# Moving two matmul operands by 64 and 128 bytes in SBUF

## The chip, the core and the metric

The kernel runs on one core of a Trainium2 chip. The metric is the time on the device in microseconds, from the first to the last work of the program; the median of three runs is given. A profile of one further execution shows what each engine did.

## The reference

The inputs are q, k and v with 8 batches, 12 heads, 448 positions and a head size of 64, and two weight matrices of 768 x 2048 and 2048 x 768. Attention uses a sigmoid instead of a softmax, so that rows need no normalisation, and a dense layer with GELU follows:

```python
scores = q @ k.T / sqrt(64) - log(448)
attn   = 1 / (1 + exp(-scores))
x      = (attn @ v)                      # heads side by side: 3584 tokens x 768
h      = x @ w_in                        # 3584 x 2048
g      = 0.5 * h * (1 + erf(h / sqrt(2)))
out    = g @ w_out                       # 3584 x 768
```

## The kernel before, in words

**Precision.** Most products are made of three matmuls each. An operand a is split into a high part, rounded to the type fp32r, and a low part a - high. The product is then low weights x high operand, high weights x low operand, and high x high, summed in PSUM. The first batches' attention is computed with plain fp32 matmuls instead.

**Tiling.** The eight batches are processed as seven rounds: each round has the 448 tokens of one batch and 64 tokens of the remaining batch (`TOK`), 512 columns in all. A round has two stages on TensorE. In the expansion (`ffn1`, with `hidden`, lines 428 to 430) 16 output tiles are made, each out of 6 chunks of x, three matmuls per chunk: 288 matmuls of 128 x 128 weights against 128 x 512 operands. Over seven rounds each of the three lines has 672. The moving operands are `xh[:, cc]` and `xl[:, cc]`. ScalarE applies GELU twice (lines 445 and 446) and VectorE subtracts, which gives the high and low part of `g[fc]`. In the projection (`ffn2`, lines 477 to 479) 6 output tiles are made, each out of 16 tiles of g, three matmuls per tile: again 288 a round and 672 per line over all. There the moving operands are `g[fc][:, 0]` and `g[fc][:, 1]`.

**Order.** The program is written out by hand; each engine works in the order in which the code issues. `window` weaves the attention of a coming batch between the projection's matmuls, so that a few scores matmuls (lines 289 and 294, or 340 in the fp32 form) or values matmuls (386, or 356), of 448 columns, stand between runs of projection matmuls. The expansion stages have no attention between them, and neither has the projection of the last round.

**Weights.** They come from DRAM as 64-bit floats and are decoded on VectorE and ScalarE in the first round, into the tiles that g takes later (`w_in`) and into `wst`; they are then stored in scratch as fp32 and loaded again by SyncE's queue in every later round. `prepare_to` splits a unit of weights into `whl` with a cast on ScalarE (line 226) and a subtraction on VectorE (line 227). Each matmul has its own 128 x 128 weights, a slice of `whl`, loaded by TensorE while the matmul before it runs.

**Places in SBUF.** Each of the 128 partitions is one range of bytes, and the pools put their tiles into it one behind the other. The pool `const` holds, in this order, `one` (32 bytes), `xh` and `xl` (12288 bytes each) and the 16 tiles of g (4096 bytes each); the pool `sb` with everything else follows, `whl` and all of attention's tiles among it. Apart from `one` every size is a multiple of 256 bytes. In the built program x, g, the weights and attention's operands therefore all start at byte 160 of a block of 256. A tile asked for under a tag that is already known takes the buffer of that tag.

Of the kernel before, what the change touches and what calls it, by code (L numbers as in the profile page):

```python
# [9 lines left out]
F32 = mybir.dt.float32  # L10
# [7 lines left out]
P = 128  # L18
# [4 lines left out]
def tile_sigmoid_attention_gelu_ffn(  # L23
# [15 lines left out]
    NF, _, NC, _ = w_in.shape  # L39
# [13 lines left out]
    const = ctx.enter_context(tc.tile_pool(name="const", bufs=1))  # L53
# [3 lines left out]

    ctx.enter_context(tc.manual_schedule())

    one = const.tile([P, 8], F32, name="one")[:, :1]  # L60
    xh = const.tile([P, NPAIR, T], F32R, name="xh")
    xl = const.tile([P, NPAIR, T], F32R, name="xl")
    g, first_w = {}, {}

    def g_tile(fc, name, dtype=F32R):
        return const.tile([P, 2, T], dtype, tag=f"g{fc}", name=name)

    scr_in = tc.dram_tile([NF, P, NC * P], F32, name="scr_in")
    scr_out = tc.dram_tile([NO, P, NFH * P], F32, name="scr_out")
    scr_x = tc.dram_tile([2, P, NPAIR, S], F32, name="scr_x")  # L70
# [511 lines left out]
```

## Time and profile before

| | |
|---|---|
| median of 3 runs | 1219.84 us (1219.82 to 1221.88) |
| profiled execution, its own time | 1225.91 us |
| its span, first to last instruction | 1224.1 us |
| TensorE busy with matmuls | 1210.4 us |
| TensorE busy with weight loads | 961.8 us |
| ScalarE, VectorE busy | 815.5 us, 769.2 us |
| granted TensorE clock | 0.998 |
| DMA, mean rate | 141 GB/s |

PE is TensorE with its matmuls, PEld its weight loads, which run beside the matmuls; DVE is VectorE, ACT is ScalarE, POOL is GpSimd, SP is SyncE, which issues most of the transfers. A row of a group gives the line, the engine and the operation, out<-in, the shapes and the count, then busy time in us, the mean of one in ns, and the idle time before them. A matmul's duration reaches from its start to its last result; since matmuls are pipelined these durations overlap, and the distance from start to start says how fast they follow each other. A row of the timeline gives the start in us from the first instruction, the duration in us, and the instruction.

### The profile page before, as it was taken

To read this page: it belongs to the slowest core of one execution; us is meant where nothing else is said; L and a number is where in the kernel's file an instruction comes from. 1 tells how busy PE (TensorE), PEld (TensorE's weight loads), DVE (VectorE), ACT (ScalarE), POOL (GpSimd) and SP (SyncE) were. 2 spreads that over 40 slices of the span, in tenths; PEclk is the share of its full clock that TensorE was granted. 3 is DMA by queue.
4 is the path that set the end of the run, shared out by engine and by line. 5 is a ranking of instruction groups with operands and counts; after the bars stand their busy time and mean duration, and the time that the engine had idled before them with its cause. 6 is when DMAs were issued, how large, how long until landed. Compare 5 with 4: busy or idle time off the path is not lost.

```text
span 1224.1 us, 15057 instructions
## 1 busy us (share of the span) xinstructions
PE 1210.4 (99%) x5448; PEld 961.8 (79%) x5448; DVE 769.2 (63%) x1127; ACT 815.5 (67%) x1247; POOL 8.6 (1%) x18
## 2 busy tenths in 40 slices
PE   8999999999999999999999999999999999999998
PEld 4338866668888888888888888888888888888887
DVE  4777788623589734798445896447984378953420
ACT  7886576534699744899546997459984489954421
POOL 0000000000000000000000000000000000000000
PEclk9999999999999999999999999999999999999999
DMA  8994567524443135442244432345422544223330
GB/s 278 300 283 153 183 214 246 183 82 154 154 140 113 57 104 174 150 143 73 91 157 147 142 108 76 123 145 162 133 69 87 172 148 147 78 82 104 131 114 26
DMA packets 79881, 172.23 MB, mean 141 GB/s; under 512 B 24256, under 2 KB 39616, under 8 KB 79808
## 3 DMA queue, kind: packets, MB, share of 16 engines
q1 hardware_dynamic: 78080, 164.99, 42.4%
q0 software_dynamic: 1728, 6.29, 1.3%
q8 instruction: 43, 0.70, 0.2%
q14 instruction: 30, 0.25, 0.1%
HBM read 144.90 MB, written 26.35 MB: 140 GB/s over the span
## 4 chain that ended last, share of the span: by engine, by line
PE 95%; DMA 3%; DVE 1%; ACT 1%; SPq 0%; issue 0%; DVEq 0%; ACTq 0%
PE po L477 13%; PE po L478 13%; PE po L479 12%; PE ph L428 12%; PE ph L429 12%; PE ph L430 12%; PE pav L386 7%; PE sc L294 6%; PE pav L356 3%; PE sc L340 3%; DMA raw_ring<-w_in_dram 1%; PE sc_l L289 1%; DMA raw<-w_in_dram 1%; DMA qr<-q_dram 1%; DVE me_ring L117 0%; SPq L328 0%
## 5 line engine op out<-in xcount | busy, mean ns | idle before, releaser
L477 PE MATMUL po<-g,whl 128*128 128x512 f32 x672 | 263.3, 392 | 0.0
L478 PE MATMUL po<-g,whl 128*128 128x512 f32 x672 | 262.3, 390 | 0.0
L479 PE MATMUL po<-g,whl 128*128 128x512 f32 x672 | 261.9, 390 | 0.0
L428 PE MATMUL ph<-xh,whl 128*128 128x512 f32 x672 | 261.5, 389 | 0.0
L429 PE MATMUL ph<-xl,whl 128*128 128x512 f32 x672 | 261.4, 389 | 0.0
L430 PE MATMUL ph<-xh,whl 128*128 128x512 f32 x672 | 261.4, 389 | 0.0
L227 DVE TENSOR_TENSOR whl<-wst,whl 128x768 fp32r<-128x768 f32 (+1 forms) x168 | 179.6, 1072 | 65.1 <-ACT whl L226 61.9
L447 DVE TENSOR_TENSOR g<-gf,g 128x512 fp32r<-128x512 f32 x112 | 77.5, 692 | 212.0 <-ACT g L446 211.8
L445 ACT ACTIVATE gf<-ph 128x512 f32<-128x512 f32 x112 | 66.9, 597 | 199.4 <-PE ph L430 185.5
L226 ACT CAST whl<-wst 128x768 fp32r<-128x768 f32 (+1 forms) x168 | 155.4, 928 | 5.5 <-PE po L479 4.2
L477 PEld LDWEIGHTS po<-g,whl 128*128 128x128 f32 x672 | 126.2, 188 | 31.9 <-issue 8.1
L428 PEld LDWEIGHTS ph<-xh,whl 128*128 128x128 f32 x672 | 126.1, 188 | 26.9 <-issue 0.7
L479 PEld LDWEIGHTS po<-g,whl 128*128 128x128 f32 x672 | 126.1, 188 | 26.8
L430 PEld LDWEIGHTS ph<-xh,whl 128*128 128x128 f32 x672 | 126.1, 188 | 26.2
L429 PEld LDWEIGHTS ph<-xl,whl 128*128 128x128 f32 x672 | 126.1, 188 | 26.1
L478 PEld LDWEIGHTS po<-g,whl 128*128 128x128 f32 x672 | 126.2, 188 | 23.8
L314 ACT ACTIVATE a<-sc 128x896 f32<-128x896 f32 (+1 forms) x174 | 128.3, 786 | 17.3 <-PE sc L340 8.3
L308 DVE TENSOR_TENSOR al<-a,ah 128x896 fp32r<-128x896 f32 x120 | 97.8, 855 | 35.4 <-ACT ah L307 35.4
L307 ACT CAST ah<-a 128x896 fp32r<-128x896 f32 x120 | 85.7, 754 | 5.6 <-PE pav L386 4.2
L386 PE MATMUL pav<-ah,vs 128*128 128x448 f32 x240 | 87.7, 365 | 0.0
L294 PE MATMUL sc<-qs,ks 128*128 128x448 f32 x360 | 82.9, 366 | 0.0
L294 PEld LDWEIGHTS sc<-qs,ks 128*128 128x128 f32 x360 | 67.6, 188 | 6.8
(60 smaller groups left out, 1210.4 us busy)
## 6 DMA issues: line engine op xcount, KB each, us to landing
wst<-scr_in SPq DMA_DIRECT2D x96, 384.0 KB, 3.1
wst<-scr_out SPq DMA_DIRECT2D x72, 512.0 KB, 3.3
kr<-k_dram SPq DMA_DIRECT2D x30, 448.0 KB, 4.3
vr<-v_dram SPq DMA_DIRECT2D x48, 256.0 KB, 4.6
out_dram<-ob SPq DMA_DIRECT2D x42, 224.0 KB, 2.0
raw_ring<-w_in_dram SPq DMA_DIRECT2D x11, 768.0 KB, 7.0
raw_ring<-w_out_dram SPq DMA_DIRECT2D x16, 512.0 KB, 4.7
qr<-q_dram SPq DMA_DIRECT2D x36, 224.0 KB, 3.2
```

The lines of the kernel that those rows point to most:

```text
L226: nc.scalar.copy(hl[:, 0, :w], t[:, :w])
L227: nc.vector.tensor_tensor(hl[:, 1, :w], t[:, :w], hl[:, 0, :w], op=ALU.subtract)
L294: nc.tensor.matmul(o, ks[:, keys], qs, start=n == 0, stop=n == 1)
L308: nc.vector.tensor_tensor(al[t][:, c], a[t][:, c], ah[t][:, c], op=ALU.subtract)
L314: nc.scalar.activation(a, sc, AF.Sigmoid, bias=NEG_LOG_S, scale=SCALE)
L386: nc.tensor.matmul(pav[:, :S], vs[:, j, c], a, start=n == 0, stop=n == len(terms) - 1)
L428: nc.tensor.matmul(ph, wl, xh[:, cc], start=cc == 0, stop=False)
L429: nc.tensor.matmul(ph, wh, xl[:, cc], start=False, stop=False)
L430: nc.tensor.matmul(ph, wh, xh[:, cc], start=False, stop=cc == NC - 1)
L477: nc.tensor.matmul(po, wl, g[fc][:, 0], start=first, stop=False)
L478: nc.tensor.matmul(po, wh, g[fc][:, 1], start=False, stop=False)
L479: nc.tensor.matmul(po, wh, g[fc][:, 0], start=False, stop=last)
```

## The change

`one` is taken from a tile of 96 bytes instead of 32. Behind `xl` a tile of 64 bytes is asked for which nobody uses. The 16 tiles of g are asked for at once, under the tags that the later requests use, so that they lie directly behind that gap. Another unused tile of 128 bytes follows. In the built program x stands at byte 224 of a block of 256 and g at byte 32, while the weights and all other operands stay at 160; everything in the pool `sb` lies 256 bytes further on. On each engine and queue the same instructions stand in the same order as before; only their addresses, the buffers' numbers and the line numbers (five more behind the edit) differ.

```diff
-    one = const.tile([P, 8], F32, name="one")[:, :1]
+    one = const.tile([P, 24], F32, name="one")[:, :1]
     xh = const.tile([P, NPAIR, T], F32R, name="xh")
     xl = const.tile([P, NPAIR, T], F32R, name="xl")
+
+    const.tile([P, 16], F32, name="gap_g")
     g, first_w = {}, {}
 
     def g_tile(fc, name, dtype=F32R):
         return const.tile([P, 2, T], dtype, tag=f"g{fc}", name=name)
 
+    for fc in range(NF):
+        g_tile(fc, f"g_place{fc}")
+    const.tile([P, 32], F32, name="gap_w")
     scr_in = tc.dram_tile([NF, P, NC * P], F32, name="scr_in")
```

## The prediction

> **What bounds the kernel now.** I read the page's head and its chain of waits first, to see whether one engine sets the end.
>
> ```profile
> span 1224.1 us, 15057 instructions
> PE 1210.4 (99%) x5448; PEld 961.8 (79%) x5448; DVE 769.2 (63%) x1127; ACT 815.5 (67%) x1247; POOL 8.6 (1%) x18
> PE 95%; DMA 3%; DVE 1%; ACT 1%; SPq 0%; issue 0%; DVEq 0%; ACTq 0%
> ```
>
> TensorE stands for 95% of the chain that ended last, and nothing else holds more than 3% of it. A change that touches neither the number of matmuls nor their order can move the time only through the distance from one matmul's start to the next. The groups of instructions say which matmuls weigh most.
>
> ```profile
> L477 PE MATMUL po<-g,whl 128*128 128x512 f32 x672 | 263.3, 392 | 0.0
> L478 PE MATMUL po<-g,whl 128*128 128x512 f32 x672 | 262.3, 390 | 0.0
> L479 PE MATMUL po<-g,whl 128*128 128x512 f32 x672 | 261.9, 390 | 0.0
> L428 PE MATMUL ph<-xh,whl 128*128 128x512 f32 x672 | 261.5, 389 | 0.0
> L429 PE MATMUL ph<-xl,whl 128*128 128x512 f32 x672 | 261.4, 389 | 0.0
> L430 PE MATMUL ph<-xh,whl 128*128 128x512 f32 x672 | 261.4, 389 | 0.0
> ```
>
> Six groups of 672, 4032 matmuls in all, stream x (L428 to L430) or g (L477 to L479) past weights from whl: exactly the three tensors whose places change. The last column is zero, so they never wait. Their 390 ns overlap one another and are not what one costs. The cost is the distance between starts, and the timeline of TensorE shows it, here around one head of attention in the second window.
>
> ```profile
> 399.68 0.39 PE L478 MATMUL po<-g,whl 128*128 128x512 f32 x1
> ...
> 401.27 0.39 PE L479 MATMUL po<-g,whl 128*128 128x512 f32 x1
> 401.49 0.36 PE L289 MATMUL sc_l<-qs,ks 128*128 128x448 f32 x1
> 401.69 1.38 PE L294 MATMUL sc<-qs,ks 128*128 128x448 f32 x6
> 402.91 0.39 PE L477 MATMUL po<-g,whl 128*128 128x512 f32 x1
> 403.14 0.40 PE L478 MATMUL po<-g,whl 128*128 128x512 f32 x1
> 403.38 0.39 PE L479 MATMUL po<-g,whl 128*128 128x512 f32 x1
> 403.61 0.39 PE L477 MATMUL po<-g,whl 128*128 128x512 f32 x1
> 403.83 0.39 PE L478 MATMUL po<-g,whl 128*128 128x512 f32 x1
> ```
>
> From 399.68 to 401.27 there are seven steps (1.59 us, 227 ns each). The seven matmuls of 448 columns take 1.42 us from 401.49 to 402.91 (203 ns each), the first of them 200 ns. The three 512-column steps right behind attention take 0.70 us (402.91 to 403.61, 233 ns each) before the fourth is back at 220 to 230. So the same matmul on the same operands costs 227 ns in one moment and 233 ns in another.
>
> Is another engine behind that? The windows by stage say no: here the second expansion (264.9 to 330.2), the window behind it, and the last projection, which has no attention beside it.
>
> ```profile
> 264.90:330.20 65.30, 65.30 (x289) 54.05 (x288) 29.01 (x36) 32.94 (x53) 0.00 (x0) 1.00 0.44 144
> 330.20:429.90 99.70, 99.70 (x458) 85.64 (x457) 82.30 (x130) 86.95 (x136) 0.00 (x0) 1.00 0.36 114
> 1155.00:1220.10 65.10, 65.10 (x289) 53.87 (x287) 12.50 (x11) 13.49 (x17) 0.00 (x0) 1.00 0.26 85
> ```
>
> Columns are length, busy PE, PEld, DVE, ACT, POOL, then granted clock, DMA share and GB/s. Both the expansion and the last projection hold 288 matmuls: 65.3/288 = 227 ns and 65.1/288 = 226 ns, though VectorE and ScalarE are busy 29 and 33 us in one and 13 and 13 us in the other, and DMA 0.44 against 0.26. The clock is 1.00 in all three. What makes 227 or 233 ns is therefore inside TensorE, between its two readings of SBUF: the moving operand, and the weights of the next matmul. The timeline of weight loads shows how these lie together.
>
> ```profile
> 399.91 0.19 PEld L477 LDWEIGHTS po<-g,whl 128*128 128x128 f32 x1
> 400.14 0.19 PEld L478 LDWEIGHTS po<-g,whl 128*128 128x128 f32 x1
> ```
>
> The load at 399.91 starts with the third matmul of that stretch (399.68 plus 0.23) and lasts 0.19 of its 0.227 us. So each weight load lies under the matmul before it, from its start, and ends some 37 ns ahead of the next start: at 512 columns the load itself is not the bound.
>
> **The change part by part.** The first tile grows by 64 bytes, which moves xh and xl by 64. A gap of 64 bytes ahead of g moves g by 128. A gap of 128 behind g moves everything later by 256, so weights, attention's tiles and staging keep their place modulo 256. No instruction, wait or transfer is added, removed or reordered, on any engine or queue. The gaps are never written, and the placeholders for g share the buffers that g takes later. These cost nothing, and no cover is needed for it, because nothing is issued.
>
> What can change is the step of the 4032 matmuls above, 2016 with x and 2016 with g. The trace has no matmul whose operands stand at different places modulo 256, because all their tiles begin at one place and their slices step by multiples of 256. So I bound the step from both sides.
>
> From below: the 448-column step of 200 ns against 227 ns for 512 columns gives 27/64 = 0.42 ns per column. 512 columns at 0.42 are 216 ns, and 11 ns per matmul are left over. If that whole rest were the two readings disturbing one another, and the new places ended it, 4032 x 11 ns = 44 us would go. From above: the dearest step that the same matmul shows in a run is 233 ns, 6 ns more, and 4032 x 6 ns = 24 us would come. The ends are -44 and +24 us, 1176 and 1244 us against the median.
>
> [...]
>
> Which value between? That the steps behind attention rise to 233 ns and fall back by themselves, without a wait, says that the relative timing of the two readings costs something. Since one reading walks through addresses as time goes on, a shift in address is much like a shift in time, so the places should matter. But the moving operand passes through 256 bytes in 64 columns, 64 x 0.42 = 27 ns, and so goes round some seven times under one 0.19 us load: a new starting place moves the moments of meeting more than their number. I therefore take neither end, but half of the 11 ns, and in one of the two stages only, because x and g now stand a quarter and a half of the 256 bytes away and it is unlikely that both are equally good. That is 2016 x 5.4 ns = 10.9 us.
>
> Would the gain arrive? In the window from 330.2 to 429.9 the next busiest engine is ScalarE with 86.95 of 99.7 us. Even the full 11 ns on its 288 matmuls takes 3.2 us away and leaves 96.5 us, still 9 us more than ScalarE works. So it stays TensorE's, and the transfers (0.36 of the time) have room too.
>
> The profiled execution took 1225.91 us, with a span of 1224.1 us and 1.8 us around it, and lies 6 us above the median of 1219.84. The differences here are per step, so I take them from the median: 1219.84 - 10.9 = 1209 us.
>
> **The rivals.** *Nothing changes.* The two readings may not meet by address at all: the 11 ns may be a fixed cost of a change of weights, and the 233 ns an after-effect of the shorter steps of attention. For it: the 227 ns are the same to a nanosecond over whole stages while the slices of weights and operands change. Against it: all those slices stand at the same place modulo 256, so this sameness tests nothing below 256 bytes. Time: 1219.84 us.
>
> The Trainium skill's page "SBUF — State Buffer", section "Who interferes with whom", stands on this side: TensorE has two independent read ports, one for the moving operand and one for weights, and waits for nobody. By that rule the sum would be zero and the time 1219.84. The trace agrees as to the other engines (227 and 226 ns with much and little work beside); on the two ports against each other no run here decides.
>
> *The new places are worse.* The steady 227 ns is the lowest step that 512 columns show; every disturbed one is dearer. If the common place is a lucky one, in which the weights' reading runs behind the moving one without touching it, then any shift leads into the 233 ns. This is settled in the stages of L428 and L477 themselves: in both, it costs 24 us (1244), in one alone 12 us (1232). It decides as soon as the mean step over both stages is above 227.7 ns (0.6 ns x 4032 = 2.4 us). Against it: the step recovers to 227 within four matmuls, so TensorE settles rather than drifts, and might settle at new places too.
>
> *Better in one stage, worse in the other.* With 11 ns saved in one (22 us) and 6 ns lost in the other (12 us) the time is 1210, near my own. With 5.4 saved and 6 lost it is 1221, no change.
>
> That the change misses its aim is shut out by the sizes in the diff: 32 to 96 bytes for the first tile, 64 and 128 for the gaps, all operands by a whole number of floats.
>
> **How the numbers follow.** Differences up to 0.2%, 2.4 us, cannot be told from no change in this kernel. My forecast of faster has 0.44, no change 0.26, slower 0.30 (half of it in one stage, half in both). The likeliest case alone would lie from 1190 to 1217. The range of 1188 to 1240 leaves out the last quarter of the lower bound, about 0.06, and the full 233 ns in both stages, about 0.08.
>
> **What would show it.** In the profile after, the starts of L428 to L430 in an expansion stage and of L477 to L479 in the last projection give the two steps at once: 65.3 and 65.1 us for 288 matmuls each, now. Forecast: one of them falls to about 63.7 us (221 ns) and the other stays. No change: both stay within 0.2 us. Slower: one or both near 67 us. The steps of attention (203 ns) must not change, since its operands keep their common place. If those move as well, or if the two stages stay and the time still changes, the step between the matmuls was the wrong place to look.

## The result: 1.5% slower, and the profile after

The changed kernel takes 1238.62 us (median of four runs, 1237.59 to 1239.33) against 1220.31 us before: a ratio of 1.0147, with a 95% interval of 1.013 to 1.0165. The forecast of 1209 us was wrong in its sign. The time lies between the two prices given for the rival "the new places are worse" (1232 for one stage, 1244 for both).

The head of the page of the changed kernel, with its chain of waits:

```profile
span 1235.8 us, 15057 instructions
PE 1225.8 (99%) x5448; PEld 963.3 (78%) x5448; DVE 770.2 (62%) x1127; ACT 816.2 (66%) x1247; POOL 8.8 (1%) x18
PE 97%; ACT 2%; DMA 0%; issue 0%; SPq 0%; ACTq 0%
```

The same instructions, and the other engines have the same work (VectorE 770.2 against 769.2 us, ScalarE 816.2 against 815.5). Only TensorE has become busier, by 15.4 us. The windows by stage answer to those of before; the columns are length, busy PE, PEld, DVE, ACT, POOL, clock, DMA share and GB/s. They are the second expansion, the window behind it and the last projection:

```profile
261.10:327.00 65.90, 65.90 (x289) 54.07 (x288) 28.99 (x36) 33.06 (x53) 0.00 (x0) 1.00 0.45 143
327.00:428.70 101.70, 101.70 (x457) 85.81 (x457) 82.41 (x130) 87.00 (x136) 0.00 (x0) 1.00 0.36 112
1165.00:1231.90 66.90, 66.90 (x289) 54.08 (x287) 12.50 (x11) 13.49 (x17) 0.00 (x0) 1.00 0.25 83
```

The expansion grew from 65.3 to 65.9 us (x, 64 bytes), the last projection from 65.1 to 66.9 (g, 128 bytes), and the window with attention in it from 99.7 to 101.7. The timeline of TensorE around one head of attention shows it matmul by matmul (start in us, duration):

```profile
573.74 0.39 PE L482 MATMUL po<-g,whl 128*128 128x512 f32 x1
...
574.89 0.40 PE L484 MATMUL po<-g,whl 128*128 128x512 f32 x1
575.13 0.37 PE L294 MATMUL sc_l<-qs,ks 128*128 128x448 f32 x1
575.34 1.40 PE L299 MATMUL sc<-qs,ks 128*128 128x448 f32 x6
576.58 0.39 PE L482 MATMUL po<-g,whl 128*128 128x512 f32 x1
```

Five projection steps take 1.15 us (230 ns each), the step into attention 0.24, and the seven steps of attention 1.45 us (575.13 to 576.58), where they took 1.42 before, although none of attention's operands has moved against its weights. Where the same seven stand behind an expansion stage, they still take 1.41 us in this trace (327.05 to 328.46), as they did before (1.41 us):

```profile
326.82 0.39 PE L435 MATMUL ph<-xh,whl 128*128 128x512 f32 x1
327.05 0.36 PE L294 MATMUL sc_l<-qs,ks 128*128 128x448 f32 x1
327.25 1.38 PE L299 MATMUL sc<-qs,ks 128*128 128x448 f32 x6
328.46 0.39 PE L482 MATMUL po<-g,whl 128*128 128x512 f32 x1
```

So it is what runs ahead of a seven that makes it dearer.

To sum up over the whole kernel I took all distances from start to start of the two traces, group by group. From the first expansion matmul to the last start of all,

| steps | number | before, ns | after, ns | more, us |
|---|---|---|---|---|
| expansion to expansion | 2009 | 226.7 | 229.0 | 4.5 |
| projection to projection | 1882 | 228.5 | 232.8 | 8.2 |
| projection into attention | 115 | 226.7 | 238.5 | 1.4 |
| within attention's sevens | 720 | 202.1 | 206.7 | 3.3 |
| the rest | | | | 0.1 |

Together that is 17.5 us, which is the whole difference between these two points of the traces: 1128.1 us before, 1145.6 us after. Their ends can be read from the groups' first and last starts, before and then after:

```profile
L428 PE MATMUL ph<-xh,whl x672: 389/389/500, 91.9 to 1154.3; 128*128 128x512 f32 x168
L479 PE MATMUL po<-g,whl x672: 388/389/398, 159.7 to 1220.1; 128*128 128x512 f32 x168
```

```profile
L433 PE MATMUL ph<-xh,whl x672: 388/388/501, 86.1 to 1164.4; 128*128 128x512 f32 x168
L484 PE MATMUL po<-g,whl x672: 390/393/404, 154.5 to 1231.7; 128*128 128x512 f32 x168
```

From 91.9 to 1220.1 before, from 86.1 to 1231.7 after. (In the earlier profile the first expansion began 6 us later. Of its chain of waits 3% are transfers, where the later one has 0%, and its granted clock is 0.95 from 60 to 92 us, where the later one has 1.00. These 6 us ahead of the first expansion are why the two spans differ by 11.7 us only.)

### The profile page after: what moved, and what is told of

Its sections match the earlier page's. It is cut to its first block, busy times and chain, and to the rows that moved or that the text cites. A ratio compares the mean times of both kernels' runs of the same rounds, so it can differ in the third digit from the quotient of the medians.

```text
span 1235.8 us, 15057 instructions
## 1 busy us (share of the span) xinstructions
PE 1225.8 (99%) x5448; PEld 963.3 (78%) x5448; DVE 770.2 (62%) x1127; ACT 816.2 (66%) x1247; POOL 8.8 (1%) x18
## 4 chain that ended last, share of the span: by engine, by line
PE 97%; ACT 2%; DMA 0%; issue 0%; SPq 0%; ACTq 0%
PE po L482 13%; PE po L483 13%; PE po L484 13%; PE ph L435 13%; PE ph L434 12%; PE ph L433 12%; PE pav L391 7%; PE sc L299 6%; PE sc L345 4%; PE pav L361 4%; PE sc_l L294 1%; ACT a L319 1%; ACT me_ring L135 0%; ACT me_ring L138 0%; DMA qk<-k_dram 0%; ACT a_last L319 0%
## 5 line engine op out<-in xcount | busy, mean ns | idle before, releaser
L482 PE MATMUL po<-g,whl 128*128 128x512 f32 x672 | 266.0, 396 | 0.0
L483 PE MATMUL po<-g,whl 128*128 128x512 f32 x672 | 265.5, 395 | 0.0
L484 PE MATMUL po<-g,whl 128*128 128x512 f32 x672 | 265.4, 395 | 0.0
L450 ACT ACTIVATE gf<-ph 128x512 f32<-128x512 f32 x112 | 66.9, 597 | 203.0 <-PE ph L435 188.8
```

Source lines behind the costliest of these rows:

```text
L482: nc.tensor.matmul(po, wl, g[fc][:, 0], start=first, stop=False)
L483: nc.tensor.matmul(po, wh, g[fc][:, 1], start=False, stop=False)
L484: nc.tensor.matmul(po, wh, g[fc][:, 0], start=False, stop=last)
```

## Experiments: the two shifts apart, and together with the weights

*x alone*, 64 bytes. g goes back to the weights' place:

```diff
-    const.tile([P, 16], F32, name="gap_g")
+    const.tile([P, 48], F32, name="gap_g")
-    const.tile([P, 32], F32, name="gap_w")
```

> x stands 64 bytes further on, g keeps the weights' place modulo 256. Theory (each stage pays for its own operand's place): the expansion's step is about 229.2 ns as in the changed kernel, the projection and attention go back to the values of before; 2016 x 2.4 ns = 5 us above the kernel before, about 1225 us. Rival (the two shifts act together, for instance through the writes of g and the reads of x): the time stays near 1238 us or goes back to 1220 us.

Measured: 1226.24 us against 1221.81 of the kernel before beside it, ratio 1.0039 (1.0024 to 1.0054). Its expansion and its last projection:

```profile
259.60:325.50 65.90, 65.90 (x289) 54.09 (x288) 29.00 (x36) 32.95 (x53) 0.00 (x0) 1.00 0.45 143
1153.60:1218.70 65.10, 65.10 (x288) 53.87 (x287) 12.50 (x11) 13.50 (x17) 0.00 (x0) 1.00 0.26 85
```

*g alone*, 128 bytes:

```diff
-    one = const.tile([P, 24], F32, name="one")[:, :1]
+    one = const.tile([P, 8], F32, name="one")[:, :1]
-    const.tile([P, 16], F32, name="gap_g")
+    const.tile([P, 32], F32, name="gap_g")
```

> g stands 128 bytes further on, x keeps the weights' place. Theory (each stage for itself): the projection's step is about 232 to 233 ns, the steps of attention that stand between projection matmuls are 4 ns dearer as in the changed kernel, the expansion goes back to 226.7 ns: about 13 us above the kernel before, 1233 us. Rival (acting together): 1220 or 1238 us.

Measured: 1236.07 against 1221.81 us, ratio 1.0113 (1.0088 to 1.0137). Expansion, window and last projection:

```profile
265.40:330.70 65.30, 65.30 (x289) 54.06 (x288) 28.99 (x36) 32.94 (x53) 0.00 (x0) 1.00 0.45 144
330.70:432.40 101.70, 101.70 (x457) 85.81 (x456) 82.45 (x130) 86.97 (x136) 0.00 (x0) 1.00 0.36 112
1165.90:1232.80 66.90, 66.90 (x288) 53.86 (x287) 12.50 (x11) 13.50 (x17) 0.00 (x0) 1.00 0.25 83
```

Each stage pays for its own operand: 0.4% and 1.1% add up to the 1.5% of both. The dearer attention comes with g alone, too: its steps in this trace are 206.9 ns, and 202.2 ns in that of x alone.

*Everything 64 bytes further on*: only `one` grows to 96 bytes, and x, g, the weights and attention's operands all move with it.

> x, g, the weights and all of attention's operands stand 64 bytes further on together. Theory (only the place of the moving operand relative to the weights counts): no step changes, 1220 us. Rival (the absolute place of x counts): the expansion's step is 229 ns or more, 1225 us or above.

Measured: 1222.99 against 1221.81 us, ratio 1.0005 (0.9991 to 1.0018), no difference. Its expansion:

```profile
261.70:327.00 65.30, 65.30 (x290) 54.07 (x289) 29.06 (x36) 32.94 (x53) 0.00 (x0) 1.00 0.45 144
```

So it is the distance between moving operand and weights that costs, not where x lies by itself.

## Experiments: the step by itself

These kernels leave attention and the dense layer out. They load a few tiles and run blocks of matmuls, one block behind the other without a wait. The first block of each such run begins with some 8 to 14 steps of about 427 ns and is left out. The matmul of a block, in place m of the moving operand and w of the weights:

```python
mo, wo = m // 4 + 512 * (i % 3), w // 4 + 128 * (i % 8)
nc.tensor.matmul(last[:, :cols], we[:, wo : wo + P], mv[:, mo : mo + cols], start=i == 0, stop=i == LEN - 1)
```

> No attention and no dense layer: only 35 blocks of 64 matmuls with 128 x 128 fp32r weights and a moving operand of 512 (the last four blocks 448) columns, the moving operand m bytes and the weights w bytes past a common place modulo 256 (in the tile's name), and a result that is not the reference's. Theory (relative place modulo 256): at m=0 the block takes 63 x 226.7 + 389 ns = 14.7 us, at m=64 14.8, at m=128 15.0; m=64 w=64 and m=256, m=512 are as m=0; m=0 w=64 is as m=192. Some places may be quicker than 14.7; 216 ns a step would be 14.0 us. Rival (absolute place): m=64 w=64 is as m=64. Rival (what stands around decides, not the place): all blocks of 512 columns take the same.

The groups of the trace, one a block; the busy time of a block is 63 steps and one duration:

```profile
L58 PE MATMUL aj_m128w0c512b<-mv,we 128*128 128x512 f32 x64 | 15.0, 395 | 0.0
L58 PE MATMUL af_m64w0c512b<-mv,we 128*128 128x512 f32 x64 | 14.8, 391 | 0.0
L58 PE MATMUL ay_m0w192c512b<-mv,we 128*128 128x512 f32 x64 | 14.8, 391 | 0.0
L58 PE MATMUL az_m64w64c512b<-mv,we 128*128 128x512 f32 x64 | 14.7, 390 | 0.0
L58 PE MATMUL au_m256w0c512b<-mv,we 128*128 128x512 f32 x64 | 14.7, 389 | 0.0
L58 PE MATMUL aq_m240w0c512b<-mv,we 128*128 128x512 f32 x64 | 14.7, 388 | 0.0
L58 PE MATMUL ab_m0w0c512b<-mv,we 128*128 128x512 f32 x64 | 14.7, 389 | 0.0
```

Taken over the last 32 starts of a block, the step is 226.7 ns at the common place, 229.0 at 64 bytes and 232.1 at 128: what the two stages of the changed kernel have (229.0, and 232.4 in the last projection). At 256 and 512 bytes it is 226.7 again, moving both by 64 gives 226.7, and weights moved by 192 count as an operand moved by 64. The theory of the distance modulo 256 held in all of these; the rivals are out.

> As the run of blocks before (64 matmuls of 512 columns in a block, nothing else of the computation, a result that is not the reference's), but with the places between, in steps of 4 bytes. Theory (the common place is the quietest, because the two readings then settle into a fixed pattern): no block is under 14.7 us, the many others are at 14.8 to 15.4 us. Rival (the 227 ns still hold an avoidable clash): some place gives 14.0 to 14.5 us (216 to 224 ns a step).

With this run all 64 places in steps of 4 bytes have been tried, each behind one other place. Two of the dearest, a cheap one and the common place:

```profile
L57 PE MATMUL ad_m20w0c512b<-mv,we 128*128 128x512 f32 x64 | 15.5, 404 | 0.0
L57 PE MATMUL bk_m196w0c512b<-mv,we 128*128 128x512 f32 x64 | 15.5, 403 | 0.0
L57 PE MATMUL ac_m12w0c512b<-mv,we 128*128 128x512 f32 x64 | 14.8, 390 | 0.0
L57 PE MATMUL ab_m0w0c512b<-mv,we 128*128 128x512 f32 x64 | 14.7, 389 | 0.0
```

No block is under the common place; place 240 was level with it in the first sweep, at 226.7 ns. At 20, 68, 100, 116 and 196 bytes every step is 240.0 ns. The rival that hoped for 216 to 224 ns somewhere is out, and with it the gain that I had forecast.

> Only blocks of 64 matmuls again, with a result that is not the reference's. In the names: m place of the moving operand, c its columns, k columns of weights, own: moving operand and its own weights alternate together between place 0 and 64, next: the moving operand stands where the weights of the NEXT matmul stand, h: both in bf16. Theory (the moving read meets the load of the next matmul's weights, and this costs by the lines of weights read): k=64 and k=32 steps are nearer to 216 than to 227 ns and the place matters less; 'next' gives 226.7 ns, 'own' does not (230 ns or more). Rival (a fixed cost per matmul): the step at k=32 is 227 ns as well. For bf16, half the bytes: theory says less of an effect of the place, under 3 ns between places; the rival none.

```profile
L70 PE MATMUL avnextr_m0c512k128b<-mv,we 128*128 128x512 f32 x64 | 15.1, 396 | 0.0
L70 PE MATMUL anr_m0c512k32b<-mv,we 128*32 128x512 f32 x64 | 15.0, 394 | 0.0
L70 PE MATMUL auownr_m0c512k128b<-mv,we 128*128 128x512 f32 x64 | 15.0, 394 | 0.0
L70 PE MATMUL acr_m0c504k128b<-mv,we 128*128 128x504 f32 x64 | 14.7, 388 | 0.0
L70 PE MATMUL awh_m0c512k128b<-mvb,web 128*128 128x512 bf16 x64 | 14.0, 379 | 0.0
L70 PE MATMUL azh_m64c512k128b<-mvb,web 128*128 128x512 bf16 x64 | 14.0, 379 | 0.0
```

Half of what I expected was wrong. With 32 columns of weights instead of 128 the step is not shorter but longer (231.7 ns), so the cost does not go by the amount of weights read. With the moving operand where the *next* weights stand it is 233.3 ns, where its *own* stand 231.7: neither is 226.7, so this does not tell which of the two loads matters. 504 columns take the 226.7 ns of 512, so the step does not simply follow the number of columns. And with bf16 no effect shows: 215.8 ns at all five places (0, 16, 32, 64 and 128 bytes; none between two multiples of 16, where fp32r has its dearest ones, was tried). I had expected a smaller effect.

> Blocks of 64 matmuls of 512 columns alone, with a result that is not the reference's, at 0, 64 and 20 bytes: both (as before), movestill (the moving operand repeats one column 512 times), loadstill (the weights repeat one column 128 times), bothstill, onemove (the same slice of the moving operand in every matmul), oneload (the same slice of weights in every matmul). Theory (two readings that walk through the same memory disturb each other): with either standing still the step no longer depends on the place and goes to 216 ns or near it; onemove and oneload are as both (226.7, 229, 240 ns). Rival (a property of the 4-byte type in TensorE, and not of two readings): the standing ones have 227 ns as well and still depend on the place.

```diff
+            if kind in ("movestill", "bothstill"):
+                move = mv[:, mo : mo + 1].to_broadcast([P, 512])
+            if kind in ("loadstill", "bothstill"):
+                load = we[:, wo : wo + 1].to_broadcast([P, P])
```

```profile
L61 PE MATMUL f_both20b<-mv,we 128*128 128x512 f32 x64 | 15.5, 404 | 0.0
L61 PE MATMUL l_loadstill20b<-mv,we 128*128 128x512 f32 x64 | 15.4, 402 | 0.0
L61 PE MATMUL j_loadstill0b<-mv,we 128*128 128x512 f32 x64 | 14.8, 391 | 0.0
L61 PE MATMUL i_movestill20b<-mv,we 128*128 128x512 f32 x64 | 14.0, 379 | 0.0
L61 PE MATMUL g_movestill0b<-mv,we 128*128 128x512 f32 x64 | 14.0, 379 | 0.0
```

When the moving operand repeats one column, the step is 215.8 ns at every place: the 11 ns above that, and all dependence on place, come with an fp32r operand that walks through memory. When the weights repeat one column, the step still depends on the place (228.7, 231.7 and 238.2 ns at 0, 64 and 20 bytes); there the theory had said 216 and was wrong. Reading the same slice of the operand or of the weights in every matmul changes nothing (226.7, 228.8, 240.0).

## Experiments: back in the kernel

*x 20 bytes further on*, cut out of one larger tile:

```diff
+    xs = const.tile([P, 2 * NPAIR * T + 64], F32R, name="xs")
+    xh, xl = (
+        xs[:, 5 + n * NPAIR * T : 5 + (n + 1) * NPAIR * T].rearrange("p (a b) -> p a b", b=T)
+        for n in range(2)
+    )
```

> x stands 20 bytes further on, g as in the kernel before. Theory (the blocks' steps hold in the kernel): the expansion's step is 240.0 ns, 2016 x 13.3 = 27 us more, about 1247 us. Rival (the blocks are a special case, and in the kernel places under 64 bytes don't tell): 1220 to 1225 us.

Measured: 1248.15 against 1221.94 us, ratio 1.0219 (1.02 to 1.0238), 26 us where 27 were expected. The expansion:

```profile
264.20:333.30 69.10, 69.10 (x290) 55.55 (x289) 29.22 (x38) 32.94 (x53) 0.00 (x0) 1.00 0.41 136
```

*The distances swapped*: x 128, g 64 bytes (`one` of 160 bytes, `gap_g` and `gap_w` of 192 bytes each).

> The changed kernel with the distances swapped: x 128 and g 64 bytes further on. Theory (each stage by its own operand's place, by the blocks' steps): expansion 232.2 ns (2016 x 5.5 = 11 us more), projection about 229 to 230 ns (4 to 6 us more, and some us for attention between): 1236 to 1240 us. Rival (the expansion does not mind its place as much as the projection does): expansion under 230 ns and under 1230 us in all.

Measured: 1237.74 against 1221.94 us, ratio 1.0131 (1.0111 to 1.0151). Expansion and last projection:

```profile
263.60:330.50 66.90, 66.90 (x289) 54.25 (x288) 29.06 (x36) 32.94 (x53) 0.00 (x0) 1.00 0.43 141
1167.40:1233.10 65.70, 65.70 (x288) 53.90 (x287) 12.50 (x11) 13.49 (x17) 0.00 (x0) 1.00 0.25 84
```

The two stages have changed roles, 66.9 us for the one at 128 bytes and 65.7 for the one at 64: the blocks' steps hold in the kernel at these two places, whichever operand it is.

*x 16 bytes before the weights' place*: the same cut with 4 in place of 5, a tail of 8 floats, and `one` of 256 bytes.

> x stands 16 bytes BEFORE the weights' place modulo 256 (byte 144 of a block of 256), g as in the kernel before. Theory (the place decides by the fixed pattern that the step settles into, and the blocks show the same 226.7 ns at 240 as at 0): the expansion's step stays 226.7 ns, 1220 us. Rival (only the very same place is good): 229 ns or more, 1225 us or above.

Measured: 1236.25 against 1221.94 us, ratio 1.0116 (1.0098 to 1.0135). Here the theory was wrong:

```profile
263.10:330.30 67.20, 67.20 (x290) 54.05 (x289) 29.17 (x37) 32.96 (x53) 0.00 (x0) 1.00 0.44 140
```

The steps of this second expansion are 233.3 ns on average, all at 233 or 234, though the block at the same place had settled at 226.7. The first expansion of the same run, which comes behind the plain fp32 attention, settles at 236.7. The last run asks whether the way in decides:

> Blocks of matmuls alone, with a result that is not the reference's: the place 240 (16 bytes before the weights', modulo 256), and after it the place 0, each entered from 48 matmuls at another place (0, 64, 128, 192, 224, 20, and place 0 with 448 columns). Theory (at 240 there are two patterns that repeat themselves, 226.7 and 233.3 ns, and the state on entry chooses; at 0 there is one): some of the seven blocks at 240 end at 226.7 and others at 233.3, the one entered from place 0 with 512 columns at 233.3 as in the whole kernel; all blocks at 0 end at 226.7. Rival (the whole kernel does something else to x): all blocks at 240 end at 226.7.

```profile
L58 PE MATMUL ah_m240c512b<-mv,we 128*128 128x512 f32 x64 | 15.3, 400 | 0.0
L58 PE MATMUL ad_m240c512b<-mv,we 128*128 128x512 f32 x64 | 15.1, 396 | 0.0
L58 PE MATMUL an_m0c512b<-mv,we 128*128 128x512 f32 x64 | 14.7, 390 | 0.0
L58 PE MATMUL bd_m0c512b<-mv,we 128*128 128x512 f32 x64 | 14.7, 389 | 0.0
```

It does matter. Entered from the common place, as in the kernel, place 240 settles at 233.3 ns (block ad), and from 224 too; entered from 64, 128, 192, 20 or from 448 columns it settles at 236.7; the 226.7 of the first sweep did not come again. There, too, the block before stood at 224, with 64 matmuls instead of 48, so the place before does not decide alone. With the first sweep this place has three patterns that repeat themselves, one more than I had expected, and the kernel shows two of them. It is not the only such place: a block of 48 at 64 bytes stays at 233.3 ns when it comes from place 240, and the last projection with g at 128 bytes takes 232.4 ns a step in the changed kernel and 233.3 with g moved alone. The common place, entered in the same seven ways, ends at 226.7 ns each time.

*Attention's operands 64 bytes further on.* In the first sweep 448 columns took 200.1 ns a step at 64 bytes and 202.6 at the common place, which would point to a version quicker than both kernels. I tried it on sevens between runs of 24 wide matmuls first:

> Blocks of three times 24 matmuls of 512 columns at the common place and 7 of 448 columns whose moving operand stands m bytes further on, as attention stands between the projection's matmuls; nothing else is computed, and the result is not the reference's. At m=0 the three sevens with what they leave behind cost 3 x (7 x 202.9 + 14) ns more than 72 steps of 226.7 ns: 16.3 + 4.3 = 20.8 us for a block with the last matmul's end. Theory (the step of 448 columns is 200.1 ns at 64 bytes, against 202.6): m=64 is 3 x 7 x 2.5 = 0.05 us shorter, or a little more where the steps behind also go back to 226.7 ns. Rival (seven are too few to settle): no place is shorter than m=0 by more than 0.02 us.

```profile
L59 PE MATMUL g_mix64b<-mv,we 128*128 128x512 f32 (+1 forms) x93 | 20.8, 384 | 0.0
L59 PE MATMUL c_mix0b<-mv,we 128*128 128x512 f32 (+1 forms) x93 | 20.8, 384 | 0.0
```

From first to last start, place 64 takes 20.48 us and the common place 20.40 and 20.42; the best other one, 128, has 20.40. So the rival forecast the time rightly, but not for its reason. At 64 bytes the seven settle at once: their steps are about 200 ns from the second on, and one seven, up to the start of the next wide matmul, takes 1.406 us against 1.419. What costs is left behind: nine wide steps are disturbed and together lose some 48 ns against 226.7 a step, where at the common place three lose 14 ns. None of the 15 other places tried was better than the common one, and no such version of the kernel was run.

## Why the prediction was wrong, point by point

**What bounds the kernel** was right. The step from matmul to matmul carries the whole difference: 17.5 of 17.5 us.

**"What makes 227 or 233 ns is inside TensorE, between its two readings"** was right in what matters: the distance of the two operands modulo 256 changes the step, with the other engines' work unchanged, and moving both together does not. The rival of no effect is out: 20 bytes cost 13.3 ns a step. On its side stood the Trainium skill's "SBUF — State Buffer", "Who interferes with whom", by which TensorE has two independent read ports and waits for nobody. With these fp32r operands the step does depend on how the two lie to one another; with bf16 it was the same at all five places tried, as that rule would have it.

**The bounds.** The 18.3 us measured lie between -44 and +24, but neither end was a bound. The upper one, out of the steps behind attention, was near the truth for these two places by luck: x at 20 bytes costs 13.3 ns a step, over twice the 6 ns. (Those steps are 231 to 233 ns in the trace, 5 ns more on average; 233 came from starts rounded to 10 ns.) The lower end was reached by no place tried. Its 216 ns came from the first of the seven attention steps, 200 ns; their mean of 203 would have given 24/64 = 0.375 ns a column and 192 ns. That 215.8 ns was then measured, with a standing operand and with bf16, is in part luck too. The 11 ns above it are real, but they come with the walk of an fp32r operand, and no place among the 64 removes any of them.

**The step that failed** is "I therefore take neither end, but half of the 11 ns, and in one of the two stages only". From a step that rises and falls back I concluded that the common place had something to lose its cost by. The same rows said the opposite, as the rival noted: the steady step was the lowest one that 512 columns showed, and TensorE came back to it by itself. They spoke for a settled pattern with nothing to gain in it, and the blocks bear that out: the common place ended at 226.7 ns behind each of seven entries, and no other place was lower. Moving the operand took this pattern away. In place of -5.4 ns in one stage, the runs show +2.2 ns for x and +4.3 to 5.7 ns for g.

**"It is unlikely that both are equally good"** was right (229.0 and 232.4 ns), but both are worse.

**"The steps of attention must not change"** was wrong. They went from 202.1 to 206.7 ns and carry 3.3 us. A seven takes up a pattern by the state in which it is entered. Before, its steps go from 199 ns to 207, to three of 202 or 203 and then round again, like the blocks of 448 columns with their 202.6 ns on average. Behind the moved projection they stay at 206 or 207 ns from the second step on, and behind an expansion they are as before in the very same trace. The step into attention is 12 ns longer, with g alone as well (239.2 ns). No term of the sum had either. The prediction called moving attention steps a sign that the step was the wrong place to look; that conclusion would have been wrong too, for they are steps as well and follow those ahead of them.

**The rival "the new places are worse"** was right in mechanism and place. Its price of 6 ns was nearly right for g and too high for x. That the time lies between its two prices is in part luck: the 4032 matmuls lose 12.7 us, as much as it had for one stage, though both lose, and the 4.7 us of attention come on top, which it had not priced.

What stays open is what happens inside. That the two readings disturb one another fits all this, but no run sees it directly: why 226.7 and not 215.8 ns, why a distance of 4 bytes more than a multiple of 16 is mostly the dearest, what chooses among the patterns of one place, and whether it is the load of the next or of the current weights that matters. The tries with alternating places and with 32 columns of weights did not settle that.

## What to carry to other kernels

When fp32r matmuls bound a kernel, read the distance from start to start and not the durations, and know where moving operand and weights lie modulo 256 bytes: 20 bytes ahead of one of them cost 2% here. A step that returns to its lowest value by itself after a disturbance, as this one did, is more likely a pattern worth keeping than a clash to be removed. Before moving anything, a run of bare blocks over all places prices the choice, but enter each place as the kernel enters it: the block at 240 bytes promised 226.7 ns where the kernel had 233.3. A short run of other matmuls between takes over the state around it and leaves one behind, so price it in its surroundings.

## What had not been expected of the hardware

- The step of 128 x 128 fp32r matmuls with 512 columns depends on the distance between moving operand and weights modulo 256 bytes: 226.7 ns at 0, up to 240.0 at 20, 68, 100, 116 and 196 bytes. With bf16 it is 215.8 ns at all five places tried.
- One place can have several patterns that repeat themselves, by what ran before: 226.7, 233.3 and 236.7 ns at 240 bytes, and 202.6 or 206.7 ns for attention's 448 columns at the common place.
- With the moving operand standing on one column, the step is 215.8 ns in fp32r as well; with the weights standing it is not.
- Fewer columns of weights do not shorten the step at the common place (32 columns: 231.7 ns), and 504 moving columns take as long as 512.
